# A conformer block on one core: the first query chunk of each batch by seven-product score quads

## The chip, the cores and the metric

The kernel runs on one core of a Trainium2 chip. TensorE (PE) multiplies, PEld are its weight loads, VectorE is DVE, ScalarE is ACT, GpSimd is POOL, and SyncE (SP) issues most DMAs. The metric is device time in microseconds (us), the median of several runs. About 0.2% of it, 3.7 us, can be told from no change.

## The reference, cut to what matters

B = 2 batches of T = 4000 tokens, width D = 512, bfloat16:

```python
x1 = x + 0.5 * (silu(layernorm(x) @ w_ff1_a) @ w_ff1_b)
h = layernorm(x1)
q, k, v = h @ w_q, h @ w_k, h @ w_v
p = softmax(einsum('btd,bsd->bts', q, k) * D ** -0.5)   # every query against all 4000 keys of its batch
x2 = x1 + einsum('bts,bsd->btd', p, v) @ w_o
# then: gated pointwise convolution, depthwise convolution of 3 taps, batch norm, silu, pointwise: x3
x4 = x3 + 0.5 * (silu(layernorm(x3) @ w_ff2_a) @ w_ff2_b)
return layernorm(x4)
```

## The kernel before, in words

**Stages.** The 8000 tokens are cut into 16 chunks of 512 (`NCK`), 8 per batch (`TCB`); the last of each batch (7 and 15) is 416 wide. First the whole first feed-forward, then `attention` (L2063) over the chunks, with the convolution stage of earlier chunks put between its matmuls (from chunk 2 on; chunk 0 has none of it), then the rest of the convolution and the second feed-forward.

**Attention.** For each query chunk `g`, `attention` steps `kt` through the batch's 32 key tiles of 128 keys (`KT`; the last has 32 keys, the "tail", done by `tail_scores`, L2244). The scores of a step go into PSUM banks named s0 to s2 in the profile, ScalarE takes their exponential into `sums`, DVE adds pairs of these (`pair_sums`, L1830), and the products with the values (PV, `pv` L1850, `pv_join` L1884) add up in banks y0 to y3. Both products use seven-product forms where they can.

**Scores in two ways.** Plain scores (`scores` L1775, `exp_pair` L1818) take 4 matmuls of 512 columns per key tile and one exponential. In chunks 0 and 8 (`plain`, `g % TCB == 0`) all 31 full tiles are plain, in a ring of three banks. In the other 14 chunks tiles 0, 1 and 30 are plain, and the 28 tiles 2 to 29 go as seven quads (`QUADS`) of four tiles. `score_quad` (L2006) computes a quad, a 2x2 block product, by seven products of 4 matmuls of 256 columns, in four steps, each with operations of other engines between:

- step 0: fifth product into s1, ScalarE copies it away (`m5`, an f32 tile that the profile calls xt); first product into s0, ScalarE copies it into s2 (`s<-s`)
- step 1: sixth product on top in s2; DVE adds m5 and writes s1 (`s<-s,xt`, the first addition); second product into s0 and its exponential
- step 2: seventh product on top in s2; DVE adds m5 again, in place in m5 (`xt<-s,xt`, the second addition); third product into s1; exponentials of s1 and m5
- step 3: fourth product on top in s2; its exponential

So the first product, the copy and the sixth form a chain, and so do the sixth, the first addition and the third, the sixth and the seventh (both through bank s2, which DVE reads between), and the seventh, the second addition and the fourth. The sums of query tiles that the products need are made by `q_sums` (L1972, 4 DVE subtractions per chunk). The sums of key tiles are the same for all chunks of a batch: `k_sums` (L1986) makes them, 4 DVE operations of 128x512 and a store to DRAM (`kfd`) per quad, the last of the four in place in the key tile; `k_stream` (L2001) loads them back for each quad of later chunks. The buffer `KF` holds the sums of two quads and alternates.

**When.** `forms` (L2101) calls these by step: in a plain chunk the form sums of quad q at kt = 4q + 6 and 4q + 7, after the plain scores of those tiles; in the others a load every fourth step. `keys_swap` (L2211) brings the keys of batch 1 in during chunks 7 and 8, one `key_queries` (transposing DMAs) every 1.625 steps. `conv_weights` (L2422, 4 DVE operations of 128x1024), called by `quads` (L2855) in `program` (L2741), makes the sums of the convolution's weights in chunk 0.

**Order.** All operations are recorded through `Sync.op` (L437) into a planner, `Plan` (L112). It has a cost for each operation (L135), takes nothing for a table load on ScalarE (`tables`, L223), and lays the operations out by simulating the engines, six times over (`run` L254, `once` L276): on TensorE the work that is ready first, then the earliest, at most 8 us ahead of the program's order (`beside`); the others by the time at which their result is due, at most 16 us ahead. The best layout is emitted as a fixed order per engine, with semaphore waits (`emit_op` L442). An engine works its queue in this order, so that a waiting operation holds those behind it.

Of the kernel before, what the change touches and what calls it, by code (L numbers as in the profile page):

```python
# [19 lines left out]
TCB = -(-T // CHUNK)  # L20
FC = F // 128
NCK = B * TCB
# [6 lines left out]
QUADS = 7  # L29
HC, HD, HF = CHUNK // 2, D // 2, FC // 2  # L30
KT = -(-T // 128)
# [10 lines left out]
def width(c):  # L42

    return CHUNK if c % TCB < TCB - 1 else T - (TCB - 1) * CHUNK
# [515 lines left out]
class Conformer:  # L560
# [1425 lines left out]
    def k_sums(self, g, q, step):  # L1986
# [11 lines left out]
                                 (s4, a12, s2, ALU.subtract, b2, b4), (a21, a11, a21, ALU.subtract, [], b_x[1::2]))[step]  # L1998
        S.op("DVE", lambda e: e.tensor_tensor(out=out, in0=u, in1=v, op=op), reads=rd + b_x, writes=wr)

    def k_stream(self, g, q):  # L2001
        n, b = (QUADS * g + q) % 2, g // TCB
        self.load(self.KF[n].rearrange("p m u j k -> p (m u j k)"), self.kfd[b][q], self.b_KF[n],
                  reads=[self.b_kfd[b][q]])
# [58 lines left out]
    def attention(self, old, hook, between):  # L2063

        S = self.S
        for g in range(NCK):
            W, plain = width(g), g % TCB == 0
            for kt in range(KT):
                if plain:
                    self.ring = [0, 1, 2]  # L2070
                else:
                    self.ring, self.rings["S"] = list(self.ASIDE.get(kt, (0, 1))), 0
                if plain and kt < KT - 1 or kt < 2 or kt == KT - 2:
                    ps, b_ps = self.scores(g, kt, None if plain else self.bank((0, 2)[kt] if kt < 2 else 0))
                    if kt < KT - 2:
                        self.exp_pair(g, kt, ps, b_ps)
                    else:
                        self.act(self.P30[:, 0:W], ps[:, 0:W], AF.Exp, [b_ps], [self.b_P30], scale=SCALE)
                elif not plain and kt < KT - 2:
                    S.front(1000)  # L2080
                    self.score_quad(g, *divmod(kt - 2, 4))
                    S.front(0)
                if g == 0 and kt < 2:
                    self.pop(old // 2 if kt == 0 else old - old // 2)
                if kt == (21 if g == 0 else 24 if g < NCK - 1 else 16):
                    self.tail_scores(g)
                if g:
                    self.units_late(g - 1, kt)
                between(g, kt)
                self.units(g, kt)  # L2090
                self.next_queries(g, kt, 9 if g else 0)
                hook(g, kt)
                self.forms(g, kt)
                self.keys_swap(g, kt)
                self.tick()
# [4 lines left out]

    def forms(self, g, kt):  # L2101

        plain, more = g % TCB == 0, g + 1 < NCK and (g + 1) % TCB
        if more and 27 <= kt < 31:
            self.q_sums(g + 1, kt - 27)
        q, r = divmod(kt - 6, 4)
        if plain:
            if 0 <= q < QUADS and r < 2:
                for n in (2 * r, 2 * r + 1):
                    self.k_sums(g, q, n)  # L2110
                if r:
                    self.after(2, lambda: self.k_sums(g, q, 4))
            if kt == 30:
                self.k_stream(g + 1, 0)
        else:
            q, r = divmod(kt + 3, 4)
            if r == 0 and (q < QUADS or more) and q > 1:
                self.k_stream(g + q // QUADS, q % QUADS)
            if kt == 1 and g % TCB == 1:
                self.k_stream(g, 1)  # L2120
        if g:
            if kt == 2:
                self.v_stream(g, 1)
            j, r = divmod(kt + 1, 4)
            if r == 0 and 1 < j < GROUPS:
                self.v_stream(g, j)
        if kt == KT - 1 and g + 1 < NCK:
            self.v_stream(g + 1, 0)
# [82 lines left out]
    def keys_swap(self, g, kt):  # L2211

        at = g * KT + kt
        if g == 0:
            steps = [(1, n) for n in range(5)] if kt == 3 else []
            j, r = divmod(kt + 1, 4)
            if 1 < j < GROUPS:
                steps += {0: [(j, 0)], 1: [(j, 1)], 2: [(j, 3)], 3: [(j, 2), (j, 4)]}[r]
            for j, n in steps:
                self.v_here(j, n)  # L2220
            if kt == 25:
                self.S.op("POOL", lambda e: e.memset(self.Vs[1], 0.0), writes=[self.b_Vs[1]])
            if kt in (26, 27):
                self.v_rest(kt - 26)
        i, r = divmod(at - KT - 4, 10)
        if 0 <= i < PAIRS:
            for n in {0: (0,), 4: (1, 2), 5: (3, 4), 8: (5,)}.get(r, ()):
                self.v_ahead(i, n)
        if TCB - 1 <= g <= TCB:
            at -= (TCB - 1) * KT  # L2230
            for k in range(KT):
                if (6 + k * (2 * KT - 12) // KT if k < KT - 1 else KT + 6) == at:
                    self.key_queries(1, k)
            for j in range(GROUPS):
                if at == KT + 3 + (j if j < 2 else 3 * (j - 1)):
                    self.v_back(j, 0)
                if at == KT + 14 + j:
                    self.v_back(j, 1)
            if at in (KT + 11, KT + 12):
                self.key_values(1, KT - 2 + at - KT - 11)  # L2240
            if at in (KT + 18, KT + 19):
                self.v_rest(at - KT - 18)
# [498 lines left out]
    def program(self, any_score):  # L2741
        i = self.i
        self.any_score = any_score
        S = self.S
# [47 lines left out]
        def ff1(c):  # L2792
            def hook(f):
# [18 lines left out]
                if c == NCK - 1:  # L2812
                    for n in {2: (0,), 4: (1,), 7: (2,), 8: (3,), 9: (4,), 10: (5,), 11: (7,), 12: (8,), 13: (9, 6), 14: (10,)}.get(f, ()):
                        self.wa_ahead(i["w_ff2_a"], n)
                    self.load_rest(f, 2)
                    if f >= FC - TPC:
                        self.fetch_queries(0, 0, f - FC + TPC)

# [15 lines left out]
        for dc in range(DC):  # L2834
            self.q_group(0, 0, dc)
            if not any_score:
                self.tick()
        if not any_score:
            for n in (0, 1, 2, 3, 4):
                self.v_here(0, n)  # L2840
        self.pop(1)
# [11 lines left out]
            return any_score or t == TCB - 1  # L2853

        def quads(g, kt):  # L2855
            if g == 0 and kt in WEIGHTS:
                self.conv_weights(WEIGHTS.index(kt))
            if g == TCB + 1 and kt == 10:
                self.conv_weights(3)
            if g - 1 in (TCB - 1, tail) and kt == 10:  # L2860
                self.conv_reload()
            if 0 <= g - 1 < tail and not plain(g - 1) and kt in TOKENS:
                self.conv_sums(TOKENS.index(kt))
            t = g - 2
            if 0 <= t < tail and not plain(t):
                for n, step in CONV.get(kt, ()):
                    self.conv_quad(t, n, step)
                if t and kt in TAPS:
                    self.taps_beside(t - 1, TAPS.index(kt))
# [181 lines left out]
        for ti in all_t:  # L3051
            ps, b_ps = banks[ti]
# [110 lines left out]
```

## Time and profile before

| | |
|---|---|
| median of 3 runs | 1860.43 us (1859.39 to 1860.77) |
| the profiled execution | 1859.74 us |
| its span on the core | 1854.8 us |
| mean granted TensorE clock | 0.999 |
| instructions | 39946 |
| attention's first chunk | about 410 to 461 us of the span |
| batch 1's first chunk | about 888 to 949 us |

The span is the time between the first and the last instruction in the trace; the rest of the execution lies around it. Every engine instruction goes through one helper and is put down to line L95, so groups are told apart by tile names (output <- inputs) and shapes. `x16` behind a row is the number of instructions joined in it. A bracket at the end of a timeline row is idle time before it and what released it.

### The profile page before, as it was taken

To read this page: it belongs to the slowest core of one execution; us is meant where nothing else is said; L and a number is where in the kernel's file an instruction comes from. 1 tells how busy PE (TensorE), PEld (TensorE's weight loads), DVE (VectorE), ACT (ScalarE), POOL (GpSimd) and SP (SyncE) were. 2 spreads that over 40 slices of the span, in tenths; PEclk is the share of its full clock that TensorE was granted. 3 is DMA by queue.
4 is the path that set the end of the run, shared out by engine and by line. 5 is a ranking of instruction groups with operands and counts; after the bars stand their busy time and mean duration, and the time that the engine had idled before them with its cause. 6 is when DMAs were issued, how large, how long until landed. Compare 5 with 4: busy or idle time off the path is not lost.

```text
span 1854.8 us, 39946 instructions
## 1 busy us (share of the span) xinstructions
PE 1840.5 (99%) x15838; PEld 1490.4 (80%) x15838; DVE 1429.7 (77%) x3090; ACT 1349.4 (73%) x2388; POOL 140.5 (8%) x356
## 2 busy tenths in 40 slices
PE   9999999999999999999999999999999999999998
PEld 6888888866878787888677788778875888888887
DVE  8889998868566777666766667766778988888896
ACT  6887777754656777678666877787768778778776
POOL 3000000000000000000000000000011000000000
PEclk9999999999999999999999999999999999999999
DMA  8333344287545655457944435543475222221211
GB/s 202 84 90 87 81 113 99 67 256 228 161 135 141 173 162 157 116 143 161 251 139 132 133 97 118 141 121 109 121 217 169 57 70 72 66 58 48 61 35 57
DMA packets 312518, 228.47 MB, mean 123 GB/s; under 512 B 191154, under 2 KB 283125, under 8 KB 312068
## 3 DMA queue, kind: packets, MB, share of 16 engines
q1 hardware_dynamic: 311796, 225.59, 44.9%
q8 instruction: 126, 2.06, 0.5%
q14 instruction: 68, 0.56, 0.1%
q10 hardware_dynamic: 528, 0.26, 0.0%
HBM read 128.99 MB, written 55.82 MB: 100 GB/s over the span
## 4 chain that ended last, share of the span: by engine, by line
PE 96%; DVE 2%; ACT 1%; DMA 0%; issue 0%; SPq 0%; DVEq 0%
PE y L95 50%; PE s L95 46%; DVE work L95 1%; ACT work L95 1%; ACT keys L95 0%; DMA xt<-in_x_dram 0%; DMA work<-work 0%; ACT sums L95 0%; DVE wff L95 0%; ACT wff L95 0%; DVE xt L95 0%; DVE sums L95 0%; DVE keys L95 0%; DVE s L95 0%; ACT s L95 0%
## 5 line engine op out<-in xcount | busy, mean ns | idle before, releaser
L95 ACT ACTIVATE sums<-s 128x512 bf16<-128x512 f32 (+4 forms) x505 | 295.2, 585 | 135.5 <-PE s L95 131.6
L95 DVE TENSOR_TENSOR sums<-sums 128x512 bf16<-128x512 bf16 (+3 forms) x528 | 202.3, 400 | 87.3 <-ACT sums L95 75.7
L95 ACT ACTIVATE keys<-s 128x512 bf16<-128x512 f32 (+3 forms) x275 | 157.0, 574 | 134.4 <-PE s L95 110.8
L95 PE MATMUL y<-work,keys 128*128 128x256 bf16 x1920 | 244.4, 273 | 0.3 <-DVE work L95 0.3
L95 PE MATMUL s<-work,keys 128*128 128x256 bf16 (+5 forms) x1456 | 225.1, 292 | 0.3 <-ACT sums L95 0.2
L95 PE MATMUL s<-sums 128*128 128x256 bf16 (+1 forms) x1428 | 212.5, 272 | 0.3 <-DVE s L95 0.3
L95 ACT ACTIVATE work<-xt,work 128x512 bf16<-128x512 bf16 x268 | 205.2, 785 | 7.4 <-DVE work L95 5.6
L95 PE MATMUL y<-wff,keys 128*128 128x256 bf16 (+3 forms) x1592 | 209.3, 276 | 0.0
L95 PEld LDWEIGHTS y<-work,keys 128*128 128x128 bf16 x1920 | 187.7, 98 | 23.0 <-DVE work L95 0.6
L95 PE MATMUL y<-sums,keys 128*128 128x256 bf16 (+1 forms) x1440 | 204.1, 270 | 0.0
L95 PE MATMUL y<-work,wff 128*128 128x256 bf16 (+3 forms) x1308 | 195.2, 272 | 0.9 <-ACT keys L95 0.8
L95 DVE TENSOR_TENSOR keys<-keys 128x1024 bf16<-128x1024 bf16 (+2 forms) x262 | 170.4, 664 | 26.1 <-ACT keys L95 17.8
L95 PEld LDWEIGHTS y<-wff,keys 128*128 128x128 bf16 (+1 forms) x1592 | 151.2, 98 | 30.1 <-issue 3.3
L95 DVE BATCH_NORM_STATS2 work<-xt 128x6 f32<-128x512 bf16 x251 | 163.1, 682 | 2.5 <-DMA xt<-in_x_dram 1.8
L95 PEld LDWEIGHTS y<-sums,keys 128*128 128x128 bf16 x1440 | 138.1, 98 | 27.1 <-issue 3.1
L95 PEld LDWEIGHTS s<-work,keys 128*128 128x128 bf16 (+1 forms) x1456 | 118.4, 97 | 49.6 <-ACT sums L95 2.4
L95 PEld LDWEIGHTS s<-sums 128*128 128x128 bf16 x1428 | 139.0, 98 | 22.7 <-DVE s L95 0.6
L95 POOL TENSOR_TENSOR work<-work 128x4 f32<-128x4 f32 (+3 forms) x107 | 91.3, 856 | 767.6 <-DVE work L95 755.2
L95 PE MATMUL y<-sums,xt 128*128 128x256 bf16 (+1 forms) x960 | 145.2, 270 | 0.0
L95 PEld LDWEIGHTS y<-work,wff 128*128 128x128 bf16 x1308 | 126.1, 98 | 18.4 <-issue 1.5
L95 DVE TENSOR_TENSOR s<-s,xt 128x512 f32<-128x512 f32 (+1 forms) x98 | 67.6, 690 | 94.7 <-PE s L95 65.3
L95 PE MATMUL s<-work 128*128 128x512 bf16 (+4 forms) x545 | 130.6, 374 | 2.4 <-DVE work L95 2.1
(155 smaller groups left out, 3236.1 us busy)
## 6 DMA issues: line engine op xcount, KB each, us to landing
xt<-kfd SPq DMA_DIRECT2D x98, 384.0 KB, 3.3
xt<-v12d SPq DMA_DIRECT2D x105, 256.0 KB, 3.1
xd<-xt SPq DMA_DIRECT2D x28, 512.0 KB, 3.6
xt<-xd SPq DMA_DIRECT2D x28, 512.0 KB, 4.4
out_dram<-xt SPq DMA_DIRECT2D x14, 512.0 KB, 2.9
xt<-in_x_dram SPq DMA_DIRECT2D x13, 512.0 KB, 4.3
dcvd<-wff SPq DMA_DIRECT2D x48, 128.0 KB, 3.5
keys<-dcvd SPq DMA_DIRECT2D x12, 512.0 KB, 4.0
```

Source lines behind the costliest of these rows:

```text
L95: return getattr(eng, self.name)(*self.args, **self.kw)
```

## The change

All 16 chunks take quads for tiles 2 to 29. In chunks 0 and 8 the form sums of a quad are therefore made ahead of it (`k_here`, new): those of quads 0 and 1 of batch 0 in the last chunk of the first feed-forward (a call at f = 5, 7, 9 and 11), those of batch 1 at the end of chunk 7, and those of quads 2 to 6 at kt = 4q - 2 and 4q - 1 of the chunk itself, straight into the buffer `KF` from which they are used, with no load. The query sums of chunk 0 are made right after its queries, those of chunk 8 at the end of chunk 7. The tail scores of chunk 0 are at step 24 and not 21, the convolution's weight sums in chunk 1 and not 0, and the keys of batch 1 come every 1.375 steps. The planner lays the whole program out anew, so that the order of instructions is another one in all attention chunks.

Per chunk 112 matmuls of 512 columns go and 196 of 256 come, with 14 copies on ScalarE and 14 additions and 4 query sums on DVE. The number of exponentials, of DMAs and of POOL operations is the same.

```diff
--- before.py
+++ after.py
@@ -1998,6 +1998,13 @@
                                  (s4, a12, s2, ALU.subtract, b2, b4), (a21, a11, a21, ALU.subtract, [], b_x[1::2]))[step]
         S.op("DVE", lambda e: e.tensor_tensor(out=out, in0=u, in1=v, op=op), reads=rd + b_x, writes=wr)
 
+    def k_here(self, g, q, half):
+
+        for n in (2 * half, 2 * half + 1):
+            self.k_sums(g, q, n)
+        if half:
+            self.after(2, lambda: self.k_sums(g, q, 4))
+
     def k_stream(self, g, q):
         n, b = (QUADS * g + q) % 2, g // TCB
         self.load(self.KF[n].rearrange("p m u j k -> p (m u j k)"), self.kfd[b][q], self.b_KF[n],
@@ -2064,25 +2071,22 @@
 
         S = self.S
         for g in range(NCK):
-            W, plain = width(g), g % TCB == 0
+            W = width(g)
             for kt in range(KT):
-                if plain:
-                    self.ring = [0, 1, 2]
-                else:
-                    self.ring, self.rings["S"] = list(self.ASIDE.get(kt, (0, 1))), 0
-                if plain and kt < KT - 1 or kt < 2 or kt == KT - 2:
-                    ps, b_ps = self.scores(g, kt, None if plain else self.bank((0, 2)[kt] if kt < 2 else 0))
+                self.ring, self.rings["S"] = list(self.ASIDE.get(kt, (0, 1))), 0
+                if kt < 2 or kt == KT - 2:
+                    ps, b_ps = self.scores(g, kt, self.bank((0, 2)[kt] if kt < 2 else 0))
                     if kt < KT - 2:
                         self.exp_pair(g, kt, ps, b_ps)
                     else:
                         self.act(self.P30[:, 0:W], ps[:, 0:W], AF.Exp, [b_ps], [self.b_P30], scale=SCALE)
-                elif not plain and kt < KT - 2:
+                elif kt < KT - 2:
                     S.front(1000)
                     self.score_quad(g, *divmod(kt - 2, 4))
                     S.front(0)
                 if g == 0 and kt < 2:
                     self.pop(old // 2 if kt == 0 else old - old // 2)
-                if kt == (21 if g == 0 else 24 if g < NCK - 1 else 16):
+                if kt == (24 if g < NCK - 1 else 16):
                     self.tail_scores(g)
                 if g:
                     self.units_late(g - 1, kt)
@@ -2100,24 +2104,17 @@
 
     def forms(self, g, kt):
 
-        plain, more = g % TCB == 0, g + 1 < NCK and (g + 1) % TCB
-        if more and 27 <= kt < 31:
+        if g + 1 < NCK and 27 <= kt < 31:
             self.q_sums(g + 1, kt - 27)
-        q, r = divmod(kt - 6, 4)
-        if plain:
-            if 0 <= q < QUADS and r < 2:
-                for n in (2 * r, 2 * r + 1):
-                    self.k_sums(g, q, n)
-                if r:
-                    self.after(2, lambda: self.k_sums(g, q, 4))
-            if kt == 30:
-                self.k_stream(g + 1, 0)
-        else:
-            q, r = divmod(kt + 3, 4)
-            if r == 0 and (q < QUADS or more) and q > 1:
-                self.k_stream(g + q // QUADS, q % QUADS)
-            if kt == 1 and g % TCB == 1:
-                self.k_stream(g, 1)
+        q, r = divmod(kt + 2, 4)
+        if r < 2:
+            if g % TCB == 0 and 1 < q < QUADS:
+                self.k_here(g, q, r)
+            if g == TCB - 1 and q >= QUADS:
+                self.k_here(g + 1, q - QUADS, r)
+        q, r = divmod(kt + 3, 4)
+        if r == 0 and 1 < q and (g % TCB if q < QUADS else (g + 1) % TCB):
+            self.k_stream(g + q // QUADS, q % QUADS)
         if g:
             if kt == 2:
                 self.v_stream(g, 1)
@@ -2229,7 +2226,7 @@
         if TCB - 1 <= g <= TCB:
             at -= (TCB - 1) * KT
             for k in range(KT):
-                if (6 + k * (2 * KT - 12) // KT if k < KT - 1 else KT + 6) == at:
+                if (6 + k * (2 * KT - 20) // KT if k < KT - 1 else KT + 6) == at:
                     self.key_queries(1, k)
             for j in range(GROUPS):
                 if at == KT + 3 + (j if j < 2 else 3 * (j - 1)):
@@ -2813,6 +2810,8 @@
                     for n in {2: (0,), 4: (1,), 7: (2,), 8: (3,), 9: (4,), 10: (5,), 11: (7,), 12: (8,), 13: (9, 6), 14: (10,)}.get(f, ()):
                         self.wa_ahead(i["w_ff2_a"], n)
                     self.load_rest(f, 2)
+                    if 4 <= f < 12 and f % 2 and not any_score:
+                        self.k_here(0, (f - 4) // 4, (f - 4) % 4 // 2)
                     if f >= FC - TPC:
                         self.fetch_queries(0, 0, f - FC + TPC)
 
@@ -2836,6 +2835,8 @@
             if not any_score:
                 self.tick()
         if not any_score:
+            for n in range(4):
+                self.q_sums(0, n)
             for n in (0, 1, 2, 3, 4):
                 self.v_here(0, n)
         self.pop(1)
@@ -2853,7 +2854,7 @@
             return any_score or t == TCB - 1
 
         def quads(g, kt):
-            if g == 0 and kt in WEIGHTS:
+            if g == 1 and kt in WEIGHTS:
                 self.conv_weights(WEIGHTS.index(kt))
             if g == TCB + 1 and kt == 10:
                 self.conv_weights(3)
```

## Prediction

> **What bounds the kernel now.** I read the page's header and busy shares first, then its chain that ended last. Columns of the second line: engine, busy us, share, instructions.
>
> ```profile
> span 1854.8 us, 39946 instructions
> ...
> PE 1840.5 (99%) x15838; PEld 1490.4 (80%) x15838; DVE 1429.7 (77%) x3090; ACT 1349.4 (73%) x2388; POOL 140.5 (8%) x356
> ...
> PEclk9999999999999999999999999999999999999999
> ...
> PE 96%; DVE 2%; ACT 1%; DMA 0%; issue 0%; SPq 0%; DVEq 0%
> ```
>
> The chain is TensorE's for 96% of the span, at full clock. So the change is worth the time of the matmuls it removes, less whatever TensorE then waits. The profiled execution took 1859.74 us, 4.9 more than its span; the median of the runs shown is 1860.43. I add the sum to the profiled execution and 0.7 us for the median. About 0.2%, 3.7 us, is what a measurement of this kernel can tell from no change.
>
> Busy time overlaps in a pipelined TensorE, so a matmul's price is the distance between starts. Timeline of TensorE, in the first feed-forward (303 matmuls of 256 columns lie between these two starts) and before the first scores (columns: start, us, operation, count):
>
> ```profile
> 199.62 1.80 PE L95 MATMUL y<-work,keys 128*128 128x256 bf16 x15
> ...
> 232.69 1.04 PE L95 MATMUL y<-work,keys 128*128 128x256 bf16 x8
> ```
>
> ```profile
> 405.22 3.62 PE L95 MATMUL s<-work 128*128 128x512 bf16 x16
> 408.67 1.46 PE L95 MATMUL y<-wff,sums 128*128 128x512 bf16 x6
> 409.97 1.89 PE L95 MATMUL s<-work,keys 128*128 128x512 bf16 x8
> 411.69 0.81 PE L95 MATMUL y<-wff,sums 128*128 128x512 bf16 x3
> ```
>
> 33.07/303 = 109.1 ns for 256 columns; 3.45/16 = 215.6 ns for 512.
>
> **Term 1, the matmuls.** In chunks 0 and 8 the change turns 28 key tiles of 4 matmuls of 512 columns into 7 quads of 28 matmuls of 256. Per chunk: 112 x 215.6 = 24.15 us against 196 x 109.1 = 21.38, so 2.77 saved; in both chunks **-5.5 us**, 0.30%. All else is about how much of this is waited away.
>
> The 168 more weight loads hide while they stay shorter than a matmul's pace (98 against 109.1 ns; I cost them at nothing, and if none hid, 168 x 98 ns = 16.5 us):
>
> ```profile
> L95 PEld LDWEIGHTS s<-work,keys 128*128 128x128 bf16 x1200 | 114.7, 98 | 45.9 <-DVE xt L95 1.8 <-issue 0.6 <-ACT wff L95 0.3
> ```
>
> The Trainium skill speaks against this trade: "TensorE: Matmul & The Clock Gate", section "Back-to-back issue gap", gives about 81 ns per matmul at 128 columns and 131 ns at 512, sustained. By it (an estimate, 98 ns at 256 between its two figures) 224 x 131 = 29.3 us would become 392 x 98 = 38.4, 9 us slower. The rows above, 215.6 and 109.1 ns, disagree.
>
> **Term 2, what a quad needs.** A quad is a chain over three engines. Timeline of a steady quad in chunk 1; TensorE's products by their buffers (xt with bank s2 is the sixth, xt,keys the seventh and then the fourth, work,keys the first), the two DVE additions, ScalarE's copy s<-s:
>
> ```profile
> 495.27 0.61 PE L95 MATMUL s<-xt 128*128 128x256 bf16 x4
> ...
> 495.99 0.70 DVE L95 TENSOR_TENSOR s<-s,xt 128x512 f32<-128x512 f32 x1
> ...
> 496.81 0.60 PE L95 MATMUL s<-xt,keys 128*128 128x256 bf16 x4
> ...
> 497.52 0.69 DVE L95 TENSOR_TENSOR xt<-s,xt 128x512 f32<-128x512 f32 x1 [0.83 <-PE s L95]
> ...
> 498.34 0.60 PE L95 MATMUL s<-xt,keys 128*128 128x256 bf16 x4
> ...
> 499.21 0.60 PE L95 MATMUL s<-work,keys 128*128 128x256 bf16 x4
> ...
> 499.91 0.58 ACT L95 ACTIVATE s<-s 128x512 f32<-128x512 f32 x1 [0.34 <-PE s L95]
> ...
> 500.55 0.61 PE L95 MATMUL s<-xt 128*128 128x256 bf16 x4
> ```
>
> The sixth product (495.27), first addition and seventh product (496.81) take 1.54 us; seventh, second addition, fourth (498.34) 1.53; first product (499.21), copy, sixth (500.55) 1.34. Here other matmuls stand between, so TensorE never stops. Where the order puts fewer between, it stops for the difference. That such stops are real, chunk 15 shows: after two matmuls of 208 columns (0.18 us at this pace) it waits 1.00, after four (0.35) 0.86:
>
> ```profile
> 1353.77 0.34 PE L95 MATMUL y<-sums,xt 128*128 128x208 bf16 x2
> 1354.77 0.52 PE L95 MATMUL s<-xt 128*128 128x208 bf16 x4 [0.67 <-ACT sums L95]
> ...
> 1355.48 0.52 PE L95 MATMUL y<-sums,keys 128*128 128x208 bf16 x4
> 1356.34 0.53 PE L95 MATMUL s<-xt 128*128 128x208 bf16 x4 [0.33 <-ACT s L95]
> ```
>
> I then counted, in the order of instructions of the built kernel, the matmuls between these products in every quad.
>
> **Term 3, chunk 0.** It has no convolution work to fill with. ScalarE at its start, before the change:
>
> ```profile
> 411.07 1.28 ACT L95 ACT_TABLE_LOAD   x1 [1.60 <-PE s L95]
> 412.37 1.63 ACT L95 ACTIVATE sums<-s 128x512 bf16<-128x512 f32 x3
> ```
>
> The exponential's table is loaded 1.10 us after tile 0's scores start (409.97), the first exponential starts at 2.40 and ends at about 3.0. Three banks of scores hide that now. After the change:
> - The first product needs tile 0's bank. The order puts 9 matmuls of 512 and 4 of 256 columns ahead of it, 2.38 us; it can start at 3.03: **0.65**.
> - The sixth waits for the copy, fourth on ScalarE (three operations of (1.63 - 0.60)/2 = 0.5 us after 2.40, so 3.9 to 4.5); TensorE is there at 3.03 + 1.09: **0.38**.
> - The seventh stands 10 matmuls, 1.09 us, behind the sixth; it needs 1.5 (the quad above): **0.4**.
> - The second addition stands on DVE behind a form sum of quad 3, which waits until quad 1's fifth product has left its buffer; that one is 18 matmuls (1.96 us) behind the seventh. Product (there at 6.0 + 1.96, done 0.6 later), sum (0.42) and addition (0.70) end at 9.7; the fourth, 24 matmuls behind the seventh, is reached at 8.6 (3.03 + 1.09 + 0.38 + 1.5 + 24 x 0.109): **1.1**. A PV product behind it waits for a pair sum on the same queue: **0.55**.
> - Quads 1 to 3 and 5 keep 1.5 us everywhere: at most 0.2.
> - Quad 4 has 8 matmuls (0.87 us) both from first to sixth and from sixth to seventh: 0.5, with 0.3 more as normalisation stands ahead of the copy on ScalarE, and **0.63**. Quad 6 has 0.87 from sixth to seventh: **0.63**.
>
> In all about **+5.3**. Rows behind the DVE side (windows: PE, PEld, DVE, ACT, POOL busy, clock, DMA share, GB/s; chunk 0, chunks with conv work, chunk 8; then groups of chunk 0 and of the second window):
>
> ```profile
> 410.00:461.00 51.00, 51.00 (x335) 30.68 (x334) 38.75 (x102) 26.46 (x44) 2.50 (x19) 1.00 0.80 237
> 579.00:641.00 62.00, 62.00 (x539) 50.10 (x538) 42.77 (x98) 45.77 (x83) 3.58 (x16) 1.00 0.54 151
> 888.00:949.00 61.00, 60.80 (x441) 39.12 (x438) 40.67 (x102) 41.20 (x74) 4.30 (x21) 1.00 0.91 242
> ```
>
> ```profile
> L95 DVE TENSOR_TENSOR keys<-keys 128x512 bf16<-128x512 bf16 x13 | 5.5, 422 | 0.8 <-PE s L95 0.7
> ...
> L95 DVE TENSOR_TENSOR xt<-xt,wff 128x1024 bf16<-128x1024 bf16 x1 | 0.7, 684 | 0.0
> ```
>
> ```profile
> L95 DVE TENSOR_TENSOR s<-s,xt 128x512 f32<-128x512 f32 x7 | 4.9, 706 | 8.5 <-PE s L95 6.4 <-ACT work L95 1.4 <-ACT xt L95 0.7
> L95 DVE TENSOR_TENSOR xt<-s,xt 128x512 f32<-128x512 f32 x7 | 4.8, 689 | 1.9 <-PE s L95 1.9
> ```
>
> ```profile
> L95 ACT ACTIVATE xt<-s 128x512 f32<-128x512 f32 x7 | 4.2, 596 | 2.5 <-PE s L95 2.4
> L95 ACT ACTIVATE s<-s 128x512 f32<-128x512 f32 x7 | 4.1, 585 | 1.3 <-PE s L95 1.1
> ```
>
> DVE in chunk 0: 38.75 + 14 x 0.70 + 4 query sums x 0.42 - 4 weight sums x 0.68 - 8 form sums x 0.42 = 44.1, against TensorE's 51.0 - 2.8 = 48.2: 92%, 76% before. That is why the additions come late here. ScalarE gets 14 x 0.59 = 8.3: 34.7 of 48.2, free.
>
> The Trainium skill, "ScalarE: Activation LUTs", section "What ACT_TABLE_LOAD costs", adds a drain of about 1.38 us to a load of 1.28. By it quad 0 would begin 1.4 us later and the sum be 1.4 higher; the row above, load 1.28 and first exponential 1.30 behind its start, shows no drain.
>
> **Term 4, elsewhere.**
> - Chunk 8: in quads 4 and 6 the seventh is 1.09 us behind the sixth, with one DVE operation ahead of the first addition: 0.7 each, **+1.4**. A wait of plain scores goes, 1.03 us where 6 matmuls (0.65) stand: **-0.4**.
>
> ```profile
> 931.11 0.83 PE L95 MATMUL y<-sums,keys 128*128 128x256 bf16 x6
> 932.14 1.02 PE L95 MATMUL s<-work,keys 128*128 128x512 bf16 x4 [0.20 <-ACT sums L95]
> ```
>
> - Chunks 7, 4 and 5 are reordered too: one quad each with 0.71 (416 wide, needing 1.54 x 416/512 = 1.25), 1.09 and 1.31 us: 0.54, 0.4 and 0.2, **+1.1**.
> - At nothing: the 8 form sums (3.4 us) and 2 stores moved into the last feed-forward chunk lie beside its matmuls (DVE has room as long as its share is as in the windows above; uncovered, 3.4); weight sums in chunk 1 (2.7 of DVE; DVE is 69% in the second window; uncovered, 2.7); loads of sums, tail scores and query sums, only moved. SP and POOL issue no more than before. The key transposes of batch 1 and their loads are issued 5 to 7 us earlier, in a stretch whose DMA share is 0.91: gain 0, or one late load of 0.4 us as above, up to 2; I take 0.
>
> **Sum.** -5.5 + 5.3 + 1.0 + 1.1 = +1.9; 1859.74 + 1.9 = 1861.6, as a median **1862.3 us**: no change that can be told.
>
> **Rivals.**
> - A, the stalls are not paid: TensorE's waits displace work that had to wait later, so each stop is paid once and cures the next. For it: in the quad above nothing is lost, and the whole chain has 4% outside TensorE. Against it: a stop cures only what waits for the same engine, and the listed ones lie one behind another on three. All saved, and chunk 8's wait gone: 1860.4 - 5.9 = 1854.5; half of the 7.8 us of stops (5.3 + 1.4 + 1.1): 1858.4.
> - B, slower: DVE becomes the bound of chunk 0. From where DVE's work between two first additions exceeds TensorE's work of that quad (in quad 0 6.6 us of DVE in the order against 46 matmuls, 5.0 us; in quad 4 6.85 against 6.3), every addition starts behind one more operation of 0.42, not only those listed. Eight more of the 14 additions late: 8 x 0.42 = 3.4, so 1865.7. Against it: over the whole chunk 92% is not 100.
> - C, the weight loads become the pace. A 512-column matmul covers a load of 98 ns by 215.6; one of 256 has only 11 ns to spare. From a load above 109 ns on, each of the 392 is late; half of the 168 added loads uncovered would cost 8.2 us: 1870.5. Against it stand the quad's own rows, which keep 109 ns a matmul beside the attention's traffic (four from 498.34 on end 0.60 later). The skill's page above, which makes small matmuls dear, points the same way.
>
> **How the numbers follow.** Forecast, 1860 to 1864.1: 0.45. A, below 1860: 0.25, of which 0.14 lies under 1856.7 (faster by over 0.2%). B, 1864.2 to 1867, the forecast's own upper tail with it: 0.28. C: 0.02. So faster 0.14, within 0.2% 0.56, slower 0.30. The range, 1856.4 to 1866.5, leaves out A's better half (0.12) and B's end with C (0.08).
>
> **What would show it.** Right: 224 matmuls of 512 columns fewer and 392 of 256 more, at 215.6 and 109.1 ns; waits of 0.4 to 1.1 us on TensorE within the first 10 us of chunk 0, with ACT sums, ACT s and DVE xt as releasers; chunk 0 longer by about 2.5 us (5.3 - 2.8); in quad 4 of chunk 0 a wait on DVE s. Wrong: chunk 0 shorter than before (A); waits in all its quads and DVE's idle time in that window near nothing (B); a pace off 109 (C); or a wait for key loads in chunk 8.

## The result, and the profile after

| | before | changed |
|---|---|---|
| median, measured beside each other | 1860.6 us (1859.39 to 1861.51, 4 runs) | 1871.4 us (1869.88 to 1872.75, 4 runs) |
| profiled execution | 1859.74 | 1871.35 |
| its span | 1854.8 | 1867.4 |

The ratio is 1.0056, 95% interval 1.0044 to 1.0069: slower by 0.44% to 0.69%, where 1862.3 (1856.4 to 1866.5) was forecast. The page of the changed kernel, the lines that answer to those of before:

```profile
span 1867.4 us, 40470 instructions
...
PE 1840.0 (99%) x16006; PEld 1505.0 (81%) x16006; DVE 1425.6 (76%) x3125; ACT 1318.6 (71%) x2417; POOL 145.1 (8%) x356
...
PE 94%; DVE 2%; ACT 2%; DMA 1%; SPq 0%; issue 0%; DVEq 0%; ACTq 0%
```

TensorE has 168 matmuls more and no more busy time, but is 94% of the chain and not 96%. To see where the span grew, take one event that each chunk has, the PV products of its tail (`y<-wff,keys 32*128`), and read its start off TensorE's timeline, for each kernel in its profiled execution:

| start of the tail's PV of chunk | before | changed | difference grown since the line above |
|---|---|---|---|
| (tile 0's scores of chunk 0) | 409.97 | 412.27 | 2.3 |
| 0 | 460.56 | 466.55 | 3.7 |
| 6 | 826.59 | 833.04 | 0.5 |
| 8 | 948.69 | 960.78 | 5.6 |
| 14 | 1316.60 | 1329.15 | 0.5 |
| 15 | 1369.83 | 1383.86 | 1.5 |
| (end of the span) | 1854.8 | 1867.4 | -1.4 |

So 3.7 us come in chunk 0, 5.6 in chunks 7 and 8, and 2.3 before the first scores, in a stage where the prediction had looked for nothing. Chunk 0 on TensorE (a bracket is the wait before a row; a stop is the distance of starts less the matmuls between, so a little more than the bracket):

```profile
415.33 0.61 PE L95 MATMUL s<-work,keys 128*128 128x256 bf16 x4 [0.51 <-ACT sums L95]
...
416.80 0.61 PE L95 MATMUL s<-xt 128*128 128x256 bf16 x4 [0.21 <-ACT s L95]
...
418.27 0.61 PE L95 MATMUL s<-xt,keys 128*128 128x256 bf16 x4 [0.21 <-DVE s L95]
...
422.04 0.61 PE L95 MATMUL s<-xt,keys 128*128 128x256 bf16 x4 [0.97 <-DVE xt L95]
...
423.37 0.85 PE L95 MATMUL y<-sums,xt 128*128 128x256 bf16 x6 [0.50 <-DVE sums L95]
```

These are the first, sixth, seventh and fourth product of quad 0 and the PV product behind it: stops of 0.68, 0.37, 0.37, 1.14 and 0.66 us. At the end of chunk 7 TensorE waits once for long. Its timeline, then ScalarE's (the exponential of the tail), then the SP queue's (its store, `pqd<-wff`, and the loads back, `wff<-pqd`), all of the changed kernel (SPq, with a q, is SyncE's queue of DMA issues):

```profile
888.72 0.25 PE L95 MATMUL y<-xt,keys 128*128 128x208 bf16 x1
892.22 0.29 PE L95 MATMUL y<-wff,keys 32*128 32x208 bf16 x1 [3.25 <-DMA wff<-pqd]
```

```profile
879.32 0.26 ACT L95 ACTIVATE wff<-s 128x104 bf16<-128x104 f32 x1 [0.43 <-PE s L95]
```

```profile
882.68 0.53 SPq L95 DMA_DIRECT2D xt<-v12d  x1
883.25 0.47 SPq L95 DMA_DIRECT2D kfd<-xt  x1
883.76 1.30 SPq L95 DMA_TRANSPOSE keys<-keysd  x1
885.11 0.58 SPq L95 DMA_DIRECT2D pqd<-wff  x1
885.73 2.50 SPq L95 DMA_TRANSPOSE keys<-keysd  x2
888.33 0.52 SPq L95 DMA_DIRECT2D xt<-v12d  x1
888.89 1.86 SPq L95 DMA_DIRECT2D wff<-pqd  x4
```

The exponential ends at 879.6, and its store is issued at 885.11, behind SP's other work, three key transposes of batch 1 among it (two fill the queue from 878.80 to 882.6); its loads follow at 888.89, behind two more. In the kernel before the same exponential ended at 872.45 and the store went out at 873.44, with one transpose between store and loads:

```profile
872.20 0.25 ACT L95 ACTIVATE wff<-s 128x104 bf16<-128x104 f32 x1
```

```profile
873.44 0.47 SPq L95 DMA_DIRECT2D pqd<-wff  x1
873.95 1.19 SPq L95 DMA_TRANSPOSE keys<-keysd  x1
876.07 1.77 SPq L95 DMA_DIRECT2D wff<-pqd  x4
```

### The profile page after: what moved, and what is told of

The parts are those of the page before. It is cut to its first block, busy times and chain, and to the rows that moved or that the text cites. A ratio compares the mean times of both kernels' runs of the same rounds, so it can differ in the third digit from the quotient of the medians.

```text
span 1867.4 us, 40470 instructions
## 1 busy us (share of the span) xinstructions
PE 1840.0 (99%) x16006; PEld 1505.0 (81%) x16006; DVE 1425.6 (76%) x3125; ACT 1318.6 (71%) x2417; POOL 145.1 (8%) x356
## 4 chain that ended last, share of the span: by engine, by line
PE 94%; DVE 2%; ACT 2%; DMA 1%; SPq 0%; issue 0%; DVEq 0%; ACTq 0%
PE y L95 50%; PE s L95 44%; DVE work L95 1%; ACT work L95 1%; DVE sums L95 0%; ACT sums L95 0%; SPq L95 0%; DVE s L95 0%; DVE xt L95 0%; DMA wff<-in_w_ff_a_dram 0%; DMA xt<-v12d 0%; ACT wff L95 0%; ACT keys L95 0%; DVE keys L95 0%; ACT s L95 0%
## 5 line engine op out<-in xcount | busy, mean ns | idle before, releaser
L95 ACT ACTIVATE sums<-s 128x512 bf16<-128x512 f32 (+4 forms) x491 | 285.9, 583 | 170.3 <-PE s L95 169.6
L95 DVE TENSOR_TENSOR sums<-sums 128x512 bf16<-128x512 bf16 (+3 forms) x528 | 193.3, 398 | 54.0 <-ACT sums L95 48.7
L95 PE MATMUL y<-sums,keys 128*128 128x256 bf16 (+1 forms) x1440 | 210.9, 271 | 0.0
L95 PE MATMUL s<-work,keys 128*128 128x256 bf16 (+5 forms) x1344 | 186.7, 276 | 2.1 <-ACT sums L95 1.9
L95 DVE TENSOR_TENSOR keys<-keys 128x1024 bf16<-128x1024 bf16 (+1 forms) x262 | 169.2, 662 | 17.0 <-ACT keys L95 13.0
L95 PE MATMUL s<-xt,keys 128*128 128x256 bf16 (+1 forms) x928 | 141.1, 270 | 4.8 <-DVE s L95 3.8
L95 PEld LDWEIGHTS s<-work,keys 128*128 128x128 bf16 (+1 forms) x1344 | 108.8, 97 | 34.6 <-issue 3.1
L95 DVE TENSOR_TENSOR s<-s,xt 128x512 f32<-128x512 f32 (+1 forms) x112 | 77.0, 688 | 76.3 <-PE s L95 43.3
```

The costliest lines, as they stand in the source:

```text
L95: return getattr(eng, self.name)(*self.args, **self.kw)
```

## The experiments

One thing about the program decides how they are read. The planner makes six layouts and emits the one that ends first by its own estimate. For the kernel before that is the first; for the changed kernel it is the third, which by that estimate ends 0.1 us ahead of the first. So the change did two things: what the diff says, and another layout of the whole program. "First layout" below means that the planner makes only that one (`PASSES = 1`). All times are medians of 10 or 11 runs (of 4 or 5 for the changed kernel, its second layout and the run with the early tail), with before measured beside them (1860.2 to 1861.1).

| run | us | ratio to before, 95% interval |
|---|---|---|
| changed kernel | 1871.40 | 1.0056 [1.0044, 1.0069] |
| changed, first layout | 1862.34 | 1.0010 [1.0001, 1.0019] |
| quads in chunk 8 alone, first layout | 1860.05 | 0.9996 [0.9987, 1.0005] |
| quads in chunk 0 alone, first layout | 1863.21 | 1.0015 [1.0006, 1.0024] |
| before, third layout | 1864.26 | 1.0018 [1.0009, 1.0027] |
| before, second layout | 1862.77 | 1.0011 [1.0002, 1.0020] |
| changed, second layout | 1870.76 | 1.0058 [1.0044, 1.0072] |
| changed, third layout, old key pace | 1864.66 | 1.0025 [1.0015, 1.0034] |
| changed, second layout, old key pace | 1863.33 | 1.0014 [1.0005, 1.0023] |
| changed, first layout, old key pace | 1862.79 | 1.0009 [1.0000, 1.0018] |

**The change in the layout of before.** Edit, in the changed kernel: `PASSES = 1`.

> The changed kernel emitted from the planner's first layout, the one from which the kernel before is emitted, and not from the third, which it took as the best of six. With it the order differs from before only around chunks 0, 7 and 8. Theory (stops in the quads and the late tail of chunk 7 cost the time): only what the third layout changed elsewhere goes, some 2.4 us at the head and 1.2 in chunks 4 and 5, so 1867 to 1869 us, and waits of 3 us or more on DMA wff<-pqd stay at the end of chunk 7. Rival (the other layout of the whole program cost the time, the quads are worth their 5.5 us): 1856 to 1860.

1862.34 us: 9 us of the loss are gone, and no wait on wff<-pqd is there. The rival's time did not come, for the stops of chunk 0 are still there, in sum as large. The theory had them right and the tail wrong.

**Its two halves.** Edit: `plain = g == 0`, or `plain = g == TCB`, with the old calls for that chunk.

> Quads in chunk 8 alone, chunk 0 plain as before, first layout. Theory (chunk 8 pays the late tail of chunk 7, 4 us, and about 1.6 us of stops in its quads for its 2.8 us): 1862 to 1864. Rival (the late tail was an accident of the third layout): 1858.5 to 1860.

> Quads in chunk 0 alone, chunk 8 plain with the keys of batch 1 at the pace of before, first layout. Theory (chunk 0 loses about 6 us in stops of TensorE for 2.8 us of matmuls): 1863 to 1864.5. Rival (the stops hang on the third layout): 1858 to 1859.

1860.05 and 1863.21, the rival for chunk 8 and the theory for chunk 0: chunk 8 by quads is worth nothing that can be told (-0.8 us, interval -2.4 to +0.9), chunk 0 costs 2.3 us more than before. The tail of chunk 7 is not late in either.

**The layout without the change.** Edit, in the kernel before: the third of the layouts is kept.

> The kernel before, unchanged but for being emitted from the planner's third layout. Theory (a layout is worth little by itself): within 1 us of before. Rival (the planner's first layout is the good one and any other costs, whatever the quads do): 2 to 4 us slower, with waits on TensorE at the head beyond the 4.5 us of before.

1864.26, so the rival: a layout is worth 3.4 us by itself. The head of the span, TensorE in the third layout of before and then in the changed kernel, shows the same two waits; the first layout has neither:

```profile
27.74 0.61 PE L95 MATMUL y<-work,wff 128*128 128x256 bf16 x4 [0.30 <-ACT s L95]
...
30.52 0.61 PE L95 MATMUL s<-sums 128*128 128x256 bf16 x4 [0.86 <-DVE s L95]
```

```profile
27.26 0.61 PE L95 MATMUL y<-work,wff 128*128 128x256 bf16 x4 [0.30 <-ACT s L95]
...
30.04 0.61 PE L95 MATMUL s<-sums 128*128 128x256 bf16 x4 [0.86 <-DVE s L95]
```

**The second layout of both.** Edit: the second is kept.

> The changed kernel, unchanged but for being emitted from the planner's second layout; the planner's own estimate puts it 0.5 us behind the third and the first. Theory (the layouts differ by several us on the chip and the estimate doesn't rank them; the first is the good one): 1866 to 1873. Rival (the third alone is bad, by the late tail of chunk 7): 1861.5 to 1863.5.

> The kernel before, unchanged but for being emitted from the planner's second layout (by its estimate the last but two of the first three, 5.2 us behind the first). Theory: 2 to 6 us slower than before, 1863 to 1867, in the same way as its third layout (1864.3). Rival (the third alone is bad): 1860 to 1861.5.

1870.76, as the theory had it, and 1862.77, just under its 1863. The first layout is the good one, and in both others the change costs 7 to 8 us, where it costs 1.5 in the first. In the second the long wait is another one, in chunk 8: TensorE behind DVE, DVE behind the load of the row sums, and that load behind key transposes:

```profile
911.48 1.46 PE L95 MATMUL y<-sums,keys 128*128 128x256 bf16 x6 [3.23 <-DVE wff L95]
```

```profile
910.65 0.18 DVE L95 RECIPROCAL work<-work 128x4 f32<-128x4 f32 x1 [3.47 <-DMA work<-lrowd]
```

```profile
899.15 2.91 SPq L95 DMA_TRANSPOSE work<-keysd  x1
902.11 0.59 SPq L95 DMA_DIRECT2D keys<-vhd  x1
902.75 1.19 SPq L95 DMA_TRANSPOSE keys<-keysd  x1
904.03 0.52 SPq L95 DMA_DIRECT2D kfd<-xt  x1
904.60 0.44 SPq L95 DMA_DIRECT2D work<-lrowd  x1
```

Not all of the delay lies ahead of the issue. DVE ends the row sums at 892.58, their store is issued at 897.43, the load back at 904.60, and that load lands 6.0 us after its issue.

**The tail of chunk 7 alone, in the third layout.** Edit: `kt == (16 if g in (TCB - 1, NCK - 1) else 24)`.

> The changed kernel, in its third layout as it is, with the tail scores of chunk 7 at step 16 and not 24. Theory (the 4.1 us at the end of chunk 7 are the tail's way through DRAM, whose store and loads stand behind key transposes on the SP queue): the wait on DMA wff<-pqd goes and nothing takes its place, 4 us less than the changed kernel: 1867 to 1868. Rival (the SP queue is full there, and the next load in it is late instead): 1870 to 1872, with a wait on another DMA at the start of chunk 8.

1869.84 (1.0045 [1.0031, 1.0058]), between theory and rival. The wait on wff<-pqd is gone, and others stand near its place:

```profile
880.72 0.89 PE L95 MATMUL y<-sums,xt 128*128 128x208 bf16 x8 [0.39 <-DMA xt<-v12d]
885.82 0.53 PE L95 MATMUL s<-xt,keys 128*128 128x208 bf16 x4 [1.33 <-DVE xt L95]
```

In its profiled execution chunks 7 and 8 are still 2.8 us longer than before, with no wait of over 1.4 us. So the tail was the victim and not the cause.

**The pace of the key transposes.** Edit, for all three layouts: `6 + k * (2 * KT - 12) // KT` as before; all else as changed.

> The changed kernel in its third layout, with the keys of batch 1 transposed one every 1.625 steps as before, and not every 1.375. The SP queue is busy 19.0 of 20 us from 860 to 880 us in the changed kernel, 15.4 before, and the tail of chunk 7 waits 3.4 us behind it. Theory (the faster pace of the key transposes fills the SP queue at the change of batches, and what TensorE needs next stands behind them): the wait of over 2 us goes, 3 to 5 us less, 1866.5 to 1868.5. Rival (the slower pace makes the keys late for the quads of chunk 8, which need them up to 5 steps earlier than plain scores): 1870 to 1874, with waits on keys in chunk 8.

> The same in the second layout, where the long wait was 3.2 us in chunk 8 on row sums (work<-lrowd) that took 6 us from issue to use, behind key transposes. Theory: that wait goes, 1866 to 1868. Rival: as above, 1870 to 1874.

> The changed kernel in its first layout with the old pace of the key transposes. Theory (the faster pace costs only where a transfer that TensorE needs next stands behind the transposes; in the first layout none does for long): 1861.5 to 1862.5, as the first layout with the new pace (1862.3), the rest being chunk 0's stops. Rival (the SP queue costs something everywhere): 1859 to 1861.

1864.66 and 1863.33: 6.7 and 7.4 us less (by the ratios 0.31% and 0.44%, 5.8 and 8.2), more than expected, and no wait of over 0.5 us from 870 to 950 us in either. The first layout stays at 1862.79, with 1.0009 against 1.0010. In the third layout the tail's store and loads now look like this (its exponential ended at 878.3):

```profile
878.41 1.29 SPq L95 DMA_TRANSPOSE keys<-keysd  x1
879.74 0.58 SPq L95 DMA_DIRECT2D pqd<-wff  x1
880.37 2.00 SPq L95 DMA_TRANSPOSE keys<-keysd  x1
882.46 0.53 SPq L95 DMA_DIRECT2D xt<-v12d  x1
883.71 1.74 SPq L95 DMA_DIRECT2D wff<-pqd  x4
```

1.4 us from exponential to store, 4 more to the loads, and not 5.5 and 3.8. In the second layout the reciprocal of the row sums starts at 903.51 with next to no wait (0.11): the sums end at 891.31, the store is issued 1.8 us later and not 4.9, and the load lands 3.0 us after its issue and not 6.0. In the third layout SP is still busy for some 19 of the 20 us from 860 on, as in the changed kernel. So, as far as these runs show, it is not how full the queue is, but what is issued ahead of the transfer that TensorE needs next. That the queue would be emptier was my mistake in the expectation.

**Chunk 0: which of its stops can be had.** All in the first layout. Its stops, TensorE:

```profile
413.14 0.61 PE L95 MATMUL s<-work,keys 128*128 128x256 bf16 x4 [0.51 <-ACT sums L95]
414.61 0.61 PE L95 MATMUL s<-xt 128*128 128x256 bf16 x4 [0.21 <-ACT s L95]
416.08 0.61 PE L95 MATMUL s<-xt,keys 128*128 128x256 bf16 x4 [0.43 <-DVE s L95]
437.83 0.61 PE L95 MATMUL s<-work,keys 128*128 128x256 bf16 x4 [0.51 <-ACT s L95]
439.13 1.04 PE L95 MATMUL s<-work 128*128 128x512 bf16 x4 [0.69 <-ACT sums L95]
440.94 0.60 PE L95 MATMUL s<-work,keys 128*128 128x256 bf16 x4 [0.78 <-ACT work L95]
```

Edit for the table load: `self.act(self.nr1, self.onef, AF.Exp, ...)` ahead of the query sums of chunk 0.

> The changed kernel in the first layout, with one exponential of a single element per partition more, ahead of the first scores, so that ScalarE loads the table while it has nothing else to do; the order on TensorE is the same but for a few lines. Theory (the first two stops of chunk 0, 0.68 and 0.37 us, come from the table load behind tile 0's scores): both go and the third (0.59) stays, 1.0 us less than the first layout's 1862.3, so 1861.3. Rival (the load is only the first of several things that are late there, and the next takes its place): 1862.0 to 1862.5, with stops of the same sum at the first three products.

The first two stops are gone; the first one left is this:

```profile
415.19 0.61 PE L95 MATMUL s<-xt,keys 128*128 128x256 bf16 x4 [0.43 <-DVE s L95]
```

The time is not less by an amount that can be told: 1862.47, 1.0008 [0.9999, 1.0017] against 1.0010. The mechanism is shown, its 1 us is not. In the profiled executions chunk 0 is 0.8 us shorter than in the first layout without this edit (53.48 against 54.28, from tile 0's scores to the tail's PV), and the stretch behind chunk 15 is 1.0 us longer, with a granted clock of 0.50 from 1413 to 1415 us (see the last section).

Edit for DVE: `k_sums` left out in chunk 0 for quads 2 to 6.

> The changed kernel in the first layout, without the 20 DVE operations that make the form sums of quads 2 to 6 in chunk 0 (that part of the computation is left out; their stores stay). This takes 8.4 us of DVE from chunk 0. Theory (DVE is not the bound of chunk 0; about 2 us of its 6 us of stops have a DVE operation as releaser): 1860.5 to 1861, with the stops on ScalarE and the bank of the first product left. Rival (DVE is the bound of chunk 0, and all stops there hang on it): 1857 to 1858.

1862.87, 1.0010: 8.4 us of DVE less, and nothing won, which neither theory nor rival had. The stops of the chunk stay 6.8 us in sum, at other products. So DVE is not the bound of chunk 0, and rival B of the prediction falls.

Edits for bank s0: projections at `{16: (0,), 17: (1,), 20: (2,), 21: (3,)}`, and at `{12: (0,), 16: (1,), 20: (2,), 24: (3,)}`.

> The changed kernel in the first layout, with the four query projections of chunk 1 that run in chunk 0 at steps 16, 17, 20 and 21, one each, and not one, two and one at 16, 17 and 20, so that none shares the second bank with a fifth product. Theory (three stops of 0.68, 0.85 and 0.94 us between 437 and 441 us are these projections and quad 4 passing one bank to and fro): 0.8 to 1.6 us less, 1860.8 to 1861.5. Rival (the three normalisations of 0.8 us that stand between on ScalarE make them): the three stops stay, 1862.0 to 1862.6.

> The changed kernel in the first layout, with the four query projections of chunk 1 at steps 12, 16, 20 and 24 of chunk 0, one for each quad, and not at 16, 17, 17 and 20. Theory (bank s0 is handed from TensorE to ScalarE and back for each product and projection, about 1.3 to 1.6 us each, and more than one projection beside a quad does not fit into its 5 us): the stops between 437 and 441 us fall from 2.5 us to under 1, so 1860.5 to 1861. Rival (ScalarE's normalisations make them, or each projection costs its stop wherever it is): 2.5 us of stops, spread out, 1862 to 1863.

1864.67 (1.0022 [1.0013, 1.0032]) and 1862.70 (1.0009). With all four in the one bank there are five stops between 436 and 442.5 us and not three:

```profile
436.16 0.61 PE L95 MATMUL s<-work,keys 128*128 128x256 bf16 x4 [0.25 <-ACT work L95]
437.50 0.61 PE L95 MATMUL s<-work,keys 128*128 128x256 bf16 x4 [0.73 <-ACT s L95]
438.80 1.04 PE L95 MATMUL s<-work 128*128 128x512 bf16 x4 [0.69 <-ACT sums L95]
440.53 1.04 PE L95 MATMUL s<-work 128*128 128x512 bf16 x4 [0.69 <-ACT work L95]
442.34 0.60 PE L95 MATMUL s<-work,keys 128*128 128x256 bf16 x4 [0.78 <-ACT work L95]
```

That the bank is handed to and fro is borne out (each hand-over ends on ScalarE's copy or exponential of it, and four of the five cost 0.7 us or more), but not the cure: one projection per quad leaves the three stops where they were, and both expectations of less time were wrong.

> The run before together with the early exponential, which removed the first two stops of chunk 0. Theory (what TensorE does not wait in chunk 0 is won at the end): 0.9 us less than the run before, about 1859.8, and below the kernel before. Rival (what is won in chunk 0 is waited for later, as DMA and the tail of attention run by their own time): no difference from the run before, 1860.5 to 1862.5, with the stops of chunk 0 gone and more stops behind 850 us.

With both edits 1862.88, 1.0011: the rival's time. The first two stops are gone, and TensorE loses more in the chunk, not less (9.3 us). Part of this is a new wait of 1.54 us at 440.90, for a DVE operation, and some 1.7 us are no stops at all: behind that wait the granted clock is halved for 3.4 us, and 256 columns take 213 ns.

Edit: quads in chunk 0 only for 6 <= kt < 18, with the form sums of the plain tiles after their scores.

> Chunk 8 by quads throughout, chunk 0 by quads 1, 2 and 3 alone and plain for the other tiles (those at the start, where ScalarE is late, and those beside the query projections), first layout. Quads 1 to 3 had stops of 0.1 us together in the first layout of the changed kernel. Theory (a quad saves 0.4 us wherever the order leaves its chain enough time): 1.2 us less than quads in chunk 8 alone (1860.05), 1858.5 to 1859.2. Rival (every quad in chunk 0 brings stops of its own, as there is no convolution work): 1860 to 1861.5.

1861.50 (1.0003 [0.9994, 1.0012]), the rival again: quads 1 to 3 run without stops of their own, but a PV product behind them waits, and the chunk takes 50.73 us, where before took 50.59:

```profile
444.25 0.61 PE L95 MATMUL y<-sums,xt 128*128 128x256 bf16 x4 [0.90 <-DVE xt L95]
```

**A version below before?** Edits: quads in chunk 8 alone, with `key_values` of the two last tiles five steps earlier; and, without that, with the old key pace.

> Quads in chunk 8 alone, first layout, with the two last key tiles of batch 1 (for the values) loaded five steps earlier; nearly nothing else moves. In the run with quads in chunk 8 alone the largest stop of chunk 8, 1.24 us on the first addition of quad 2 at 916.4, stands behind a memset on POOL that waits for this load, and behind DVE and ScalarE operations that wait for the memset. Theory (head of line: one late load holds the queues of three engines): the stop goes, 1858.7 to 1859.2, below the kernel before. Rival (another wait takes its place, as in chunk 0): 1859.7 to 1860.5.

> Quads in chunk 8 alone, first layout, old pace of the key transposes: the version that the runs point to, without chunk 0's stops and without the full SP queue. Theory: 2.8 us of matmuls less 1 to 2 us of stops that stay in chunk 8, 1859 to 1860. Rival (chunk 8 by quads needs the keys earlier, and waits for them): 1861 to 1863.

1859.84 (0.9997 [0.9987, 1.0006]) and 1859.73 (0.9994 [0.9985, 1.0003]). Neither is told from no change. The first doesn't test its theory: the planner left the load nearly where it was, and the wait stayed (1.16 and not 1.24 us). With the old pace one profiled execution, the slowest of its eleven, has a wait of 2.11 us on DVE at 900.94: chunk 8 stays sensitive to its transfers.

## Why the prediction was wrong

**Term 1 was right in size.** 168 matmuls more leave TensorE's busy time as it was (1840.0 against 1840.5), and the paces hold: in the changed kernel 4 matmuls of 256 columns take 0.44 us (898.06 to 898.50), 15 of 512 take 3.24 (407.74 to 410.98), 216 ns each. Rival C did not come. The Trainium skill, "TensorE: Matmul & The Clock Gate", section "Back-to-back issue gap", with 131 ns sustained at 512 columns, does not hold here.

**Terms 2 and 3 were right.** Forecast for the start of chunk 0: 0.65, 0.38, 0.4, 1.1 and 0.55; measured 0.68, 0.37, 0.37, 1.14 and 0.66. Quad 4: 1.43 forecast, 0.42, 0.40 and 0.59 measured. Chunk 0 in all: 5.3 of stops forecast, 6.0 measured (6.8 less the 0.8 that before has there). The chunk came out 3.7 us longer where 2.5 was forecast: 0.7 of stops more, and 0.4 for one product of chunk 1 that now runs ahead of the tail's PV. Chunk 8's quads 4 and 6: 0.7 each forecast, 0.83 and 0.71 measured, with one more of 1.04 in quad 2 that I had not found. Where the order of instructions put too few matmuls between two products, TensorE stopped for the difference. (One reading is off: in the rows of chunk 15 the 1.00 and 0.86 us are distances of starts; the stops are 0.82 and 0.51.) With the first layout, and with the old key pace in every layout, the whole change costs, by the ratios, 0.6 to 1.9 us beside before in the same layout; the sum had +1.9. In the first layout that agreement is in part luck: the span is 2.4 us longer (medians), chunk 0 costs 3.7 and not 2.5, chunks 7 and 8 are 0.1 longer and not 1.2 shorter, and the time outside the span is 0.9 shorter.

**What failed is one step of Term 4**, "The key transposes of batch 1 and their loads are issued 5 to 7 us earlier [...]: gain 0, or one late load of 0.4 us as above, up to 2; I take 0." Chunks 7 and 8 were forecast 1.2 us shorter and came 5.6 longer; undoing the pace alone takes 6.7 us (the tail's PV of chunk 8 then starts at 952.95 in the third layout, and chunks 7 and 8 take 121.2 us where before took 122.1). I asked whether the keys would come in time, and not who stands behind them in SP's queue. That queue was named in the step ("SP and POOL issue no more than before") but counted, not walked: a transpose holds it for 1.2 us or more, and the tail's way through DRAM passes it twice. In the first layout the step holds: there the new pace costs nothing that can be told (1862.34 against 1862.79). What was wrong is to take it without walking SP's order in the layout that was emitted.

**The second failure is what was left out.** I walked the order where the quads are, and took the rest as unchanged. The planner emitted its third layout and not its first, which costs 3.4 us in the kernel before, 2.3 to 2.8 of it at the head. The order is another one from about 27 us of the span on, in the first feed-forward and not in the attention alone, and the sum has no term for that.

So the 10.8 us, by ratios: third layout 0.18%, the quads themselves 0.07% (third layout, old pace, against before in the third layout), the faster keys 0.31%. In the second layout the same three are 0.11, 0.03 and 0.44%. That the late transfers and the pace are one cause is shown for both layouts; which transfer is the victim is the layout's accident. Rival A did not come: the 3.7 us of chunk 0 are not given back in the chunks behind it. The early table load removed the stops that it aimed at, without a gain that can be told; moving the projections did not remove theirs. Why the gain of the early table doesn't reach the end is not shown: in both profiled executions with it the clock was halved once, elsewhere, and run to run the spans of one kernel spread by 2 to 4 us, as much as the effect.

## What to carry to other kernels

When a change moves transfers, walk the issuing queue as you walk an engine: for every transfer that the bound engine needs next, list what stands ahead of it between its data being ready and its issue, and between its issue and its landing. A planner that keeps the best of several layouts by its own costs can change the whole program for a local edit; before judging the edit, run it in the layout of before. A spare-time argument ("only moved") holds for the engine that has the spare time, not for the queue behind it.

## What the runs showed of the hardware

Waits can cost TensorE more than their length. In the changed kernel, after the wait up to 892.22, the windows show a granted clock of 0.58 and 0.56 for some 3.4 us (columns as in the prediction's windows):

```profile
888.00:892.00 4.00, 0.97 (x10) 0.68 (x8) 1.24 (x5) 0.85 (x2) 0.00 (x0) 1.00 0.44 94
892.00:894.00 2.00, 1.78 (x15) 1.31 (x16) 1.25 (x4) 0.00 (x0) 0.00 (x0) 0.58 0.51 96
894.00:896.00 2.00, 2.00 (x14) 1.58 (x12) 0.55 (x3) 0.00 (x0) 0.00 (x0) 0.56 1.09 331
896.00:898.00 2.00, 2.00 (x24) 1.90 (x22) 1.92 (x7) 1.25 (x3) 0.00 (x0) 1.00 0.82 157
```

```profile
892.63 2.26 PE L95 MATMUL y<-sums,keys 128*128 128x208 bf16 x12
894.68 1.06 PE L95 MATMUL s<-xt 128*128 128x256 bf16 x4
895.54 0.71 PE L95 MATMUL y<-work,xt 128*128 128x256 bf16 x4
```

Twelve matmuls of 208 columns take 2.05 us, 171 ns each and not 89, and four of 256 take 0.86 and not 0.44: 1.4 us on top of the 3.4. The second layout shows the same after its wait of 3.23 us (0.50 from 912 to 914).

A single long wait is not needed. In all 20 traces the changes of the granted clock lie on a grid of steps of 3.41 us. Apart from the end of the program, the clock fell five times behind the first 20 us, each time to 0.50 for one step. Add up, for every step from 20 us on, the time by which starts of matmuls lie further apart than their pace (109 ns at 256 columns, 216 at 512). These are the five falls, and below them two of the steps that came nearest without one:

| run | end of the step, us | TensorE idle in it, us | longest single stop in it, us | clock in the next step |
|---|---|---|---|---|
| changed kernel | 892.33 | 3.31 | 3.31 | 0.50 |
| changed, second layout | 911.17 | 3.10 | 3.10 | 0.50 |
| apart and early table | 441.03 | 2.65 | 1.70 | 0.50 |
| quads in chunk 8 alone, old key pace | 901.61 | 2.27 | 2.27 | 0.50 |
| early table | 1412.94 | 2.15 | 0.94 | 0.50 |
| projections at 16, 17, 20, 21 | 440.26 | 2.09 | 0.85 | 1.00 |
| changed, first layout | 1414.00 | 2.07 | 0.94 | 1.00 |

Of some 10,800 steps, none with 2.09 us or less was followed by a fall, and every one with 2.15 or more was. So of two forecasts with the same sum of waits, the one whose waits stand close together is the worse. The grid lies elsewhere in each run, so a stop that costs the clock in one execution need not in the next: the four runs of the changed kernel have mean clocks of 0.998, 1.000, 0.998 and 0.999.

The Trainium skill, "TensorE: Matmul & The Clock Gate", section "What's actually happening", says that the clock halves after an idle window of about 3.4 us and comes back after as long a busy one. The two long waits and the return after 3.41 us agree; the other three falls do not, for there 2.15 to 2.65 us of idle time in a step were enough.

Nor had I expected that time outside the span differs between kernels: 4.9 to 5.3 us in most runs of before, 3.8 to 4.3 in the third layout of both kernels, 5.8 to 6.5 with quads in chunk 8 alone and the earlier `key_values`. That last run has a span 2.1 us shorter than before (medians), of which 1.0 us is lost outside it. No run here shows why.
